# Every load waits until the load 1.75 MB ahead of it has landed

## The chip, the cores and the metric

The kernel runs on one core of a Trainium2 chip. Its five instruction queues are PE (TensorE), DVE (VectorE), ACT (ScalarE), POOL (GpSimd) and SP (SyncE); SP only issues DMAs here, and 16 DMA engines move the bytes. The metric is the device time of one execution in microseconds, as the median of several runs. Before the change it is 363.97 us (three runs, 363.48 to 364.42).

## What is computed

Three layers in a row, all in fp32, on 2304 tokens: attention with a window of 64 keys (4 sequences of 576, 8 heads of 64), a soft mixture of experts (8 experts, 4 slots each), and a feed-forward layer of width 2048. The weights of the last layer arrive as 64-bit floats.

```python
def _attn_ref(q, k, v):
    scores = scale * np.matmul(q, k.transpose(0, 1, 3, 2))
    mask = (rel >= 0) & (rel < window)
    scores = np.where(mask, scores, -1000000000.0)
    attn = np.exp(scores - np.max(scores, axis=-1, keepdims=True))
    attn = attn / (np.sum(attn, axis=-1, keepdims=True) + 1e-09)
    return np.matmul(attn, v)
...
def _moe_ref(x, phi, w1, w2):
    logits = x @ phi
    ...
    slot_input = d.T @ x          # d: softmax of the logits over the tokens
    ...
        h = np.maximum(slot_input[e] @ w1[e], 0.0)
        slot_out[e] = h @ w2[e]
    ...
    return c @ slot_out           # c: softmax of the logits over the slots
...
def _moe2_ref(x, w_in, w_out):
    h = x @ w_in
    return (h * (1.0 / (1.0 + np.exp(-1.702 * h)))) @ w_out
```

## The kernel before

The order of the work is written out by hand; a scheduler only adds the semaphore waits. There are three stages.

*Attention, up to about 90 us.* The loop `for i in range(ns)` runs over 18 pieces of work, 16 units of two heads each and two for the last chunk of every sequence. Each turn emits the scores of piece i (`emit_s`, L312 and L327), the turns of the piece before (`emit_t`, L347 and L348), its product with v (`emit_pv`, L362) and its normalization, and spread over the turns the logits and the routing sums. POOL scales q (L235) and shifts v (L243 to L250) once a load has landed. In each turn SP gets a load of q and k (`load_qk`, 512 KB, for three turns later), one of v (`load_v`, 258.5 KB) and usually one or two weight tiles (`load_w`, 1 MB). Three buffers of q/k and three of v go round, so a load of these waits until PE and POOL are done with the buffer.

*Experts, up to about 131 us.* `load_w` walks through a list, 16 tiles of w1 and then 16 of w2, 1 MB each. The w1 tiles and w2 tiles 7 to 15 go to 16 slots (`w`), the first seven w2 tiles into the memory that attention leaves (`arena`). The last w2 tile comes in three loads (`PIECES`, 512, 256 and 256 KB). PE multiplies with w1 (`emit_w1`, L786) and w2 (`emit_w2`, L824); the last two tiles are taken piece by piece (`next_w2`, L883; `last_w2`, L891), and each piece of the sum is then added (L894) and turned (`so_turn`, L899).

*Feed-forward, up to the end.* 48 steps of 36 products each (`emit_o`, L1036) on PE, with the activations on ACT and DVE. w_in and w_out come in loads of 512 KB through `raw_load` (L150), at most a few at a time.

All loads are issued by SP in program order. Every DMA uses one of eight semaphores in turn (`DMAHW0` to `DMAHW7`), and a DMA that uses a semaphore again waits until the DMA before it on that semaphore, eight places earlier, has landed. Apart from this and the buffers nothing holds a load back, so several megabytes can be issued and not landed at the same time.

Of the kernel before, what the change touches and what calls it, by code (L numbers as in the profile page):

```python
# [13 lines left out]
I32 = mybir.dt.int32  # L14
# [10 lines left out]
NU = B * NHP  # L25
# [12 lines left out]

CONV_AT = {i: n for n, i in enumerate((3, 5, 7, 9, 11))}
W = (2, 1)  # L40
N_G = 5

N_WO = 1
# [25 lines left out]
def attention_softmoe_ffn(  # L69
# [12 lines left out]
    nc = tc.nc  # L82
# [15 lines left out]
    def mem(off, n):  # L98
        return arena[:, off:off + n]
# [24 lines left out]
    def wslot(dtype=F32):  # L124
        return wp.tile([128, 4, 512], dtype, tag="w", name="w")

    def dslot(i):
        return mem(2048 * i, 2048).rearrange("p (a f) -> p a f", a=4)

    w1t, w2t = [], []  # L130
    plan = [(w1t, w1, i, None if i < N_E else i - N_E) for i in range(16)]
    plan += [(w2t, w2, i, i if i < 7 else None) for i in range(16)]
# [2 lines left out]
    def load_w(n=1):  # L135
        for _ in range(n):
            if plan:
                lst, src, i, d = plan.pop()
                t = wslot() if d is None else dslot(d)
                v = src[i].rearrange("p (a f) -> p a f", a=4)  # L140
                if not plan:
                    t, v = [x.rearrange("p a f -> p (a f)").rearrange(
                        "p (c a f) -> p c a f", c=4, a=4) for x in (t, v)]
                for c in PIECES if not plan else (slice(0, 4),):
                    nc.sync.dma_start(out=t[:, c], in_=v[:, c])
                lst.append(t)


    def raw_load(raw, src):
        nc.sync.dma_start(out=raw.bitcast(I32), in_=src.bitcast(I32))  # L150

    def widths(raw):
        r = raw.bitcast(I32).rearrange("p (n two) -> p n two", two=2)
# [35 lines left out]
    def early_load(n):  # L189
        src = w_in[n] if n < FP else w_out[n - FP]  # L190
        if wide:
            raw_load(early_raw(n), src)
        else:
            nc.sync.dma_start(out=early_dst(n), in_=src)
# [8 lines left out]
    def qbuf(n):  # L203
        return ql if n == NU else qkb[(n - (n > NU)) % 3]

    def vbuf(n):
        return vl if n == NU else vb[(n - (n > NU)) % 3]
# [14 lines left out]

    def load_qk(n):
        if n < NU:
            nc.sync.dma_start(out=qbuf(n), in_=qk[n])
        else:
            nc.sync.dma_start(out=qbuf(n)[:, 0:768], in_=sq[n - NU])

    def scale_q(n, eng):
        q = qbuf(n)  # L230
# [5 lines left out]
            out=q, in0=q, scalar1=1.0 / 8.0, scalar2=1.0, op0=ALU.mult, op1=ALU.mult)  # L236

    def load_v(n):
        nc.sync.dma_start(out=vbuf(n)[:, 0:517], in_=vt[n])

    def set_ones(n):
        v = vbuf(n)
# [2 lines left out]
    def shift_v(u):  # L245
# [6 lines left out]
            scalar1=1.0, scalar2=1.0, op0=ALU.mult, op1=ALU.mult)  # L252

    load_qk(0)
    load_qk(1)
    load_v(0)
    load_qk(2)
    load_v(1)
    nc.vector.memset(mask, 0.0)
    nc.vector.memset(pa[:, 0:128], 0.0)  # L260
# [308 lines left out]
    for b in range(B):  # L569
        g = routing(b)  # L570
        logits, lmax, dexp, turn, total, slots, gather, norm, side = g
        n = NHP * b
# [39 lines left out]
    for i in range(ns):  # L612
# [44 lines left out]
        if i == L_AT:  # L657
            load_qk(NU)
            load_v(NU)
        if i < NU:  # L660
            load_qk(i + 3 + (i + 3 >= NU))
        if i in AHEAD:
            load_w(W_AT.get(i, 0))
# [6 lines left out]
        if i not in AHEAD:  # L670
            load_w(W_AT.get(i, 0))
# [10 lines left out]
        out=ml[:, 128:160], in_=pm[0:1, 0:128].rearrange("p (t s) -> p s t", t=TM), axis=AX.X,  # L682
# [5 lines left out]
    emit_pv(ns - 1)  # L688
    emit_norm(ns - 1)
    load_w(1)  # L690

    lpt = bank("s")[:, 0:256]
    mm = sp.tile([128, 3], F32, tag="mm", name="mm")

    def tail_logits(t):
# [11 lines left out]
        out=mm[:, 2:3], in0=pm[:, 0:1], scalar1=-1.0, scalar2=None, op0=ALU.mult)  # L707
# [15 lines left out]
        out=ltt, in_=lpt, func=ACTF.Exp, bias=m, scale=1.0, accum_out=ss)  # L723
# [14 lines left out]
    for c in range(2):  # L738
        for t in range(2):
# [3 lines left out]
                start=True, stop=True, tile_position=(0, 32 * g))  # L743
# [4 lines left out]
        out=rsl, in0=pm[:, 0:1], scalar1=ss, scalar2=1e-9, op0=ALU.add, op1=ALU.add)  # L748
# [3 lines left out]
        out=i4s, in0=i4m[:, 0:NS], scalar1=rsl, scalar2=None, op0=ALU.mult)  # L752
    nc.vector.scalar_tensor_tensor(
        out=acc, in0=psl, scalar=al, in1=acc, op0=ALU.mult, op1=ALU.add)
# [85 lines left out]
    def wout_load():  # L840
        f = len(wraw)
        if f == NF:
            return
        parts_for(f)
        r = ring[f // 2 % 2][:, 1024 * (f % 2):1024 * (f % 2) + 1024]
        if wide:
            raw_load(r, w_out[f])
        else:
            nc.sync.dma_start(out=r[:, 0:512], in_=w_out[f])
        wraw.append(r)  # L850
# [10 lines left out]
    def win_more():  # L861
        n = FP + len(iraw)
        if n == NF:
            return
        if n % FP == 0:
            winf.append(gp.tile([128, 4, 512], F32, tag="wi", name="wi", bufs=2))
        iraw[n] = gp.tile([128, 1024], F32, tag="iraw", name="iraw", bufs=2)
        if wide:
            raw_load(iraw[n], w_in[n])
        else:  # L870
            nc.sync.dma_start(out=win_dst(n), in_=w_in[n])
# [99 lines left out]
    def out_w(f):  # L971
        nc.scalar.copy(whi(f), wfs[f])  # L972

    def out_c(f):
        nc.vector.tensor_tensor(  # L975
            out=wlo(f), in0=wfs[f], in1=whi(f).bitcast(F32), op=ALU.subtract)
# [18 lines left out]
    def emit_h(n, act=True):  # L995
# [4 lines left out]
        for k, a in enumerate(range(ROUND * r, ROUND * r + ROUND, PIECE)):  # L1000
            ph = bank("m")
            c = sorted({a + x for x in cuts(n, k)} | ({2048} & set(range(a, a + PIECE))))
            for c, e in zip(c, c[1:]):
                nc.tensor.matmul(  # L1004
                    ph[:, c - a:e - a], mst[:, f * 128:f * 128 + 128], cT(c, e - c),
                    start=True, stop=True)
            g = gp.tile([128, PIECE], F32, tag="g", name="g", bufs=N_G)
            gh, gl = [gp.tile([128, PIECE], F32R, tag="r", name="r", bufs=N_R) for _ in range(2)]
# [61 lines left out]
    ahead = {10: [lambda: out_w(0)], 11: [lambda: out_c(0)]}  # L1070
# [155 lines left out]
```

## Time and profile before

| | us |
|---|---|
| median of three runs | 363.97 |
| the profiled execution | 363.21 |
| its span, first to last instruction | 361.30 |
| PE busy | 351.8 (97%) |
| PE weight loads busy (beside the matmuls) | 269.7 (75%) |
| DVE / ACT / POOL busy | 240.3 / 195.5 / 45.2 |

The page counts 18,180 DMA packets and 70.87 MB. Of the DMA queues, q1 carries the loads and stores (70.38 MB), q8 ("instruction", 24 packets, 0.39 MB) and q14 ("instruction", 12 packets, 0.10 MB) the instructions of the engines. TensorE's granted clock is at its full level all through.

How to read it: busy shares are means over the span. A matmul's end is modelled, so a PE that is busy 97% need not be at its peak. A wait is shown with what ended it; "issue" means that nothing the profile shows was missing. For loads the profile gives the time from issue to landing.

### The profile page before, as it was taken

How to read it: one execution, taken by the hardware profiler on the slowest of the kernel's cores; microseconds unless marked ns; L12 is line 12 of the kernel's file. 1: busy time of each engine (PE TensorE's matmuls, PEld its weight loads, DVE VectorE, ACT ScalarE, POOL GpSimd, SP SyncE). 2: the span in 40 equal slices, each digit the busy share in tenths (PEclk: the TensorE clock that was granted, in tenths of full speed). 3: DMA queues.
4: the chain of work that ended last, by engine and by line, in shares of the span. 5: the costliest groups of instructions: out<-in, count | busy, mean ns of one | idle time of the engine just before them, and what ended most of it. 6: DMA issues, size and time to landing. Idle time of an engine off the chain costs nothing.

```text
span 361.3 us, 7742 instructions
## 1 busy us (share of the span) xinstructions
PE 351.8 (97%) x3021; PEld 269.7 (75%) x3021; DVE 240.3 (67%) x527; ACT 195.5 (54%) x499; POOL 45.2 (13%) x90
## 2 busy tenths in 40 slices
PE   8999999998999999999999999999999999999995
PEld 6787787776633357888778887788886888888884
DVE  4667797975664128885767696998787886262624
ACT  2898899877314026764757454554445553333330
POOL 4366764620100000000000000000000000000000
PEclk9999999999999999999999999999999999999999
DMA  8999999999999993333130413040300000040404
GB/s 281 407 410 406 410 411 410 402 408 406 407 417 420 415 404 130 114 117 116 58 118 32 144 47 128 11 139 27 116 2 0 0 2 1 0 175 1 174 3 174
DMA packets 18180, 70.87 MB, mean 196 GB/s; under 512 B 2016, under 2 KB 2400, under 8 KB 14176
## 3 DMA queue, kind: packets, MB, share of 16 engines
q1 hardware_dynamic: 18144, 70.38, 50.6%
q8 instruction: 24, 0.39, 0.4%
q14 instruction: 12, 0.10, 0.1%
HBM read 65.65 MB, written 4.72 MB: 195 GB/s over the span
## 4 chain that ended last, share of the span: by engine, by line
PE 92%; ACT 2%; DVE 2%; issue 1%; DMA 1%; DVEq 0%; ACTq 0%
PE s L1036 18%; PE t L1036 18%; PE v L1036 18%; PE v L362 5%; PE m L1004 5%; PE m L347 5%; PE s L327 4%; PE s L786 4%; PE v L824 3%; PE s L312 2%; PE m L400 2%; ACT pa L339 1%; PE m L441 1%; PE m L491 1%; DMA rawt<-in_qk_dram 1%
## 5 line engine op out<-in xcount | busy, mean ns | idle before, releaser
L992 ACT ACTIVATE r<-m 128x384 fp32r<-128x384 f32 (+1 forms) x97 | 47.4, 492 | 80.6 <-PE m L1004 80.4
L1017 DVE TENSOR_TENSOR r<-g,r 128x384 fp32r<-128x384 f32 x96 | 51.4, 554 | 48.4 <-ACT g L992 40.0
L1036 PE MATMUL t<-w,r 128*128 128x512 f32 x288 | 75.8, 395 | 0.0
L1036 PE MATMUL s<-w,r 128*128 128x512 f32 x288 | 74.3, 393 | 0.0
L1036 PE MATMUL v<-w,r 128*128 128x512 f32 (+1 forms) x291 | 73.3, 387 | 0.0
L1036 PEld LDWEIGHTS t<-w,r 128*128 128x128 f32 x288 | 53.8, 188 | 14.8 <-issue 4.0
L1036 PEld LDWEIGHTS v<-w,r 128*128 128x128 f32 x291 | 54.4, 188 | 11.3
L1036 PEld LDWEIGHTS s<-w,r 128*128 128x128 f32 x288 | 52.6, 188 | 8.5
L992 ACT ACTIVATE g<-m 128x384 f32<-128x384 f32 x96 | 47.9, 500 | 0.0
L339 ACT ACTIVATE pa<-s,nm 128x128 f32<-128x128 f32 x140 | 40.9, 404 | 5.6 <-DVE nm L332 5.6
L332 DVE TENSOR_REDUCE nm<-s 128x4 f32<-128x512 f32 x35 | 22.5, 684 | 5.6 <-PE s L327 4.9
L1004 PE MATMUL m<-cT,w 128*128 128x384 f32 (+2 forms) x113 | 25.9, 320 | 0.0
L1004 PEld LDWEIGHTS m<-cT,w 128*128 128x128 f32 x113 | 20.8, 188 | 4.9 <-ACT g L992 0.7
L347 PE MATMUL m<-ident,pa 128*128 128x128 f32 x144 | 20.9, 283 | 0.8 <-ACT pa L339 0.4
L347 PEld LDWEIGHTS m<-ident,pa 128*128 128x128 f32 x144 | 15.6, 141 | 5.1 <-issue 1.8
L348 ACT COPY pa<-m 128x512 f32<-128x512 f32 x18 | 10.7, 596 | 10.4 <-PE m L347 10.4
L786 PE MATMUL s<-w,phis 128*32 128x512 f32 x128 | 14.6, 595 | 0.0
L972 ACT CAST w<-wf 128x512 fp32r<-128x512 f32 x15 | 9.3, 623 | 9.3 <-DVE wf L175 9.3
L381 DVE TENSOR_TENSOR arena<-v,rs 128x256 f32<-128x256 f32 x36 | 13.6, 419 | 0.6
L327 PE MATMUL s<-arena 64*64 64x128 f32 x352 | 13.8, 271 | 0.1
L975 DVE TENSOR_TENSOR w<-wf,w 128x512 fp32r<-128x512 f32 x15 | 10.3, 689 | 5.2 <-ACT w L972 5.1
L1056 DVE TENSOR_TENSOR w<-s,w 128x512 f32<-128x512 f32 x18 | 11.6, 684 | 2.8 <-PE s L1036 2.8
(218 smaller groups left out, 453.0 us busy)
## 6 DMA issues: line engine op xcount, KB each, us to landing
w<-in_w_dram SPq DMA_DIRECT2D x24, 1024.0 KB, 9.6
w<-in_w_out_dram SPq DMA_DIRECT2D x16, 512.0 KB, 3.4
arena<-in_w_dram SPq DMA_DIRECT2D x7, 1024.0 KB, 10.8
iraw<-in_w_in_dram SPq DMA_DIRECT2D x12, 512.0 KB, 3.3
arena<-in_qk_dram SPq DMA_DIRECT2D x10, 512.0 KB, 8.8
out_dram<-w SPq DMA_DIRECT2D x16, 256.0 KB, 2.1
arena<-in_vt_dram SPq DMA_DIRECT2D x13, 258.5 KB, 7.3
rawt<-in_qk_dram SPq DMA_DIRECT2D x6, 512.0 KB, 8.8
```

The lines of the kernel that those rows point to most:

```text
L327: nc.tensor.matmul(st[h][rows[j], c, :], q, k, start=False, stop=(c == 3), tile_position=(64 * h, 64 * j))
L332: nc.vector.tensor_reduce(out=nm[:, h], in_=st[h], axis=AX.X, op=ALU.max, negate=True)
L339: nc.scalar.activation(out=pb[h][:, c, :], in_=st[h][:, c, :], func=ACTF.Exp, bias=nm[:, h, c:c + 1], scale=1.0)
L347: nc.tensor.transpose(tt[:, c, :], pb[h][:, c, :], ident)
L362: nc.tensor.matmul(pvt[i][h][64 * j:64 * j + 64, c, :], ab[h][:, c, 64 * j:64 * j + 64], v, start=True, stop=True, tile_position=(0, 64 * j))
L381: nc.vector.tensor_tensor(out=o, in0=pv[h][:, :, 1 - h:65 - h], in1=rs[:, h].unsqueeze(2).to_broadcast([128, 4, 64]), op=ALU.mult)
L786: nc.tensor.matmul(ph[32 * j:32 * j + 32, :], siT[:, kk, :], w1t[4 * r + j][:, kk, :], start=(kk == 0), stop=(kk == KD - 1), tile_position ...
L992: nc.scalar.activation(out=(gh, g)[part][:, a:e], in_=ph[:, a:e], func=ACTF.Gelu_apprx_sigmoid)
L1004: nc.tensor.matmul(ph[:, c - a:e - a], mst[:, f * 128:f * 128 + 128], cT(c, e - c), start=True, stop=True)
L1017: nc.vector.tensor_tensor(out=gl, in0=g, in1=gh.bitcast(F32), op=ALU.subtract)
L1036: nc.tensor.matmul(accs[t][:, h], a[:, c], b[:, h], start=(first and k == 0), stop=(last and k == 2 and h.stop == 512))
L1056: nc.vector.tensor_tensor(out=o[:, h], in0=accs[t][:, h], in1=o[:, h], op=ALU.add)
```

## The change

A helper `start` now issues the loads of q/k, v and weights. It keeps a list of the loads issued so far with their bytes. For a new load it goes back through the list from the newest, adding up bytes; the first load that has at least `AHEAD_OF` = 1,750,000 bytes of listed loads between itself and the new one becomes a dependency: the new load's issue waits until that one has landed. `raw_load` goes through `start` as long as the list has fewer than `LAST` = 79 entries. `FREE` is 0, so the rule holds from the first load that has so much ahead of it. The load of phi is not on the list, nor are the loads after the last piece of w2 or the stores.

```diff
+AHEAD_OF = 1750000
+FREE = 0
+LAST = 79
...
+    queue = []
+
+    def start(out, in_):
+        x = nc.sync.dma_start(out=out, in_=in_)
+        ahead = 0
+        for y, n in reversed(queue):
+            if ahead >= AHEAD_OF and len(queue) >= FREE:
+                tc.add_manual_dep(x.ins, y.ins.name, mybir.DependencyInfo(
+                    mybir.DependencyClass.Sync, mybir.DependencyReason.DATA), reason="depth")
+                break
+            ahead += n
+        queue.append((x, int(np.prod([k for _, k in out.ap])) * 4))
+
...
-                    nc.sync.dma_start(out=t[:, c], in_=v[:, c])
+                    start(t[:, c], v[:, c])
...
-        nc.sync.dma_start(out=raw.bitcast(I32), in_=src.bitcast(I32))
+        (start if len(queue) < LAST else nc.sync.dma_start)(out=raw.bitcast(I32), in_=src.bitcast(I32))
...
-            nc.sync.dma_start(out=qbuf(n), in_=qk[n])
+            start(qbuf(n), qk[n])
...
-            nc.sync.dma_start(out=qbuf(n)[:, 0:768], in_=sq[n - NU])
+            start(qbuf(n)[:, 0:768], sq[n - NU])
...
-        nc.sync.dma_start(out=vbuf(n)[:, 0:517], in_=vt[n])
+        start(vbuf(n)[:, 0:517], vt[n])
```

The instructions of all five queues stay in their order; only waits on SP differ. At the end of the attention SP issues the last w1 tiles (`w` from `in_w1`), the last two v loads and the first w2 tiles (into `arena`). Before, in SP's queue:

```order
L145 DMA w_1589<-in_w1_dram 128x2048 [waits DMAHW1_49,DVE_49,Activation_49]
L239 DMA arena_78<-in_vt_dram 128x517 [waits DMAHW2_49,PE_49,Pool_49]
L239 DMA rawt_91<-in_vt_dram 128x517 [waits DMAHW3_49,PE_49,Pool_49]
L145 DMA w_1675<-in_w1_dram 128x2048 [waits DMAHW4_49,DVE_49,Activation_49]
L145 DMA w_1677<-in_w1_dram 128x2048 [waits DMAHW5_49,DVE_49,Activation_49]
L145 DMA arena_78<-in_w2_dram 128x2048 [waits DMAHW6_49]
```

and after:

```order
L136 DMA w_1589<-in_w1_dram 128x2048 [waits DMAHW4_49,DVE_49,Activation_49]
L136 DMA arena_78<-in_vt_dram 128x517 [waits DMAHW7_49,PE_49,Pool_49]
L136 DMA rawt_91<-in_vt_dram 128x517 [waits PE_49,Pool_49]
L136 DMA w_1675<-in_w1_dram 128x2048 [waits DVE_49,Activation_49]
L136 DMA w_1677<-in_w1_dram 128x2048 [waits DMAHW0_49,DMAHW5_49,DVE_49,Activation_49]
L136 DMA arena_78<-in_w2_dram 128x2048 [waits DMAHW6_49,DMAHW3_49]
```

No row moves. Where a row had the semaphore of the load eight places earlier, it now has that of a nearer load, or none where an earlier row waits for the same one. By the byte counts, `w_1677` waits for the w1 tile five loads before it (`w_1587`), and the first `arena` tile for the v load into `rawt_91`, two loads before `w_1677`.

The second place is the last w2 tile and the first w_out load behind it. SP's queue before:

```order
L145 DMA w_2004<-in_w2_dram 128x2048 [waits DMAHW4_49,PE_49]
L145 DMA w_2031<-in_w2_dram 128x1024 [waits DMAHW5_49,PE_49]
L145 DMA w_2031<-in_w2_dram 128x512 [waits DMAHW6_49]
L145 DMA w_2031<-in_w2_dram 128x512 [waits DMAHW7_49]
L150 DMA w_2091<-in_w_out_dram 128x1024 [waits DMAHW0_49,PE_49]
```

and after:

```order
L136 DMA w_2004<-in_w2_dram 128x2048 [waits DMAHW1_49,PE_49]
L136 DMA w_2031<-in_w2_dram 128x1024 [waits DMAHW2_49,PE_49]
L136 DMA w_2031<-in_w2_dram 128x512
L136 DMA w_2031<-in_w2_dram 128x512 [waits DMAHW3_49]
L166 DMA w_2091<-in_w_out_dram 128x1024 [waits PE_49]
```

Again nothing moves: the last piece of w2 now waits for the w2 tile four loads before it, and the w_out load has no wait on a DMA of its own any more.

## Rows read from the trace of the kernel before

**Rows 1.** Stretches: us, busy (x count) of PE, PEld, DVE, ACT, POOL; PEclk, DMA, GB/s.
```profile
2.00:90.00 88.00, 85.32 (x1593) 67.90 (x1593) 64.60 (x187) 70.64 (x221) 42.24 (x81) 1.00 1.02 404
...
100.00:126.00 26.00, 26.00 (x231) 8.85 (x234) 10.99 (x24) 5.60 (x10) 0.19 (x1) 1.00 1.01 418
...
150.00:200.00 50.00, 50.00 (x231) 40.66 (x230) 37.04 (x69) 33.74 (x73) 0.00 (x0) 1.00 0.27 90
```
**Rows 2.** Waits of PE: line waited for, us in total, times, longest.
```profile
PE v L362 <- issue: 1.7, 1, 1.7
```
**Rows 3.** Timeline of PE: start, us, what, [idle before, what ended it].
```profile
90.41 0.22 PE L362 MATMUL v<-arena,pl 128*64 128x65 f32 x1 [1.70 <-issue]
```
**Rows 4.** Timeline of ACT just before that stall.
```profile
87.59 0.59 ACT L348 COPY pl<-m 128x512 f32<-128x512 f32 x1
```
**Rows 5.** Two stretches from one instruction block's arrival to the next, columns as rows 1.
```profile
48.70:55.10 6.40, 6.40 (x127) 5.39 (x129) 6.16 (x19) 5.56 (x17) 5.41 (x9) 1.00 1.04 417
...
81.90:90.40 8.50, 6.81 (x123) 5.63 (x124) 4.91 (x18) 6.30 (x21) 0.21 (x2) 1.00 1.01 410
```
**Rows 6.** DMA queues (packets, MB, share): q8 79.3:79.5; q1, q14 79.5:87.7; q8 87.7:87.9.
```profile
q8 instruction: 1, 0.02, 33.8%
...
q1 hardware_dynamic: 666, 3.29, 100.3%
q14 instruction: 1, 0.01, 0.2%
...
q8 instruction: 1, 0.02, 33.7%
```
**Rows 7.** Timeline of SP's DMA issues: start, us, destination and source, count.
```profile
73.35 1.62 SPq L145 DMA_DIRECT2D w<-in_w_dram  x2
...
80.52 0.33 SPq L239 DMA_DIRECT2D rawt<-in_vt_dram  x1
80.95 0.85 SPq L145 DMA_DIRECT2D w<-in_w_dram  x2
81.85 1.08 SPq L145 DMA_DIRECT2D arena<-in_w_dram  x2
...
95.55 2.14 SPq L145 DMA_DIRECT2D arena<-in_w_dram  x3
...
103.74 0.33 SPq L145 DMA_DIRECT2D w<-in_w_dram  x1
...
115.69 0.33 SPq L145 DMA_DIRECT2D w<-in_w_dram  x1
```
**Rows 8.** Issue to landing (last number, us), issues at 73.4, 80.5, 81.0, 81.4, 81.9, 95.6, 103.7, 115.7.
```profile
w<-in_w_dram SPq DMA_DIRECT2D x1, 1024.0 KB, 8.6
...
rawt<-in_vt_dram SPq DMA_DIRECT2D x1, 258.5 KB, 5.2
...
w<-in_w_dram SPq DMA_DIRECT2D x1, 1024.0 KB, 7.3
...
w<-in_w_dram SPq DMA_DIRECT2D x1, 1024.0 KB, 9.3
...
arena<-in_w_dram SPq DMA_DIRECT2D x1, 1024.0 KB, 11.4
...
arena<-in_w_dram SPq DMA_DIRECT2D x1, 1024.0 KB, 7.7
...
w<-in_w_dram SPq DMA_DIRECT2D x1, 1024.0 KB, 6.9
...
w<-in_w_dram SPq DMA_DIRECT2D x1, 256.0 KB, 15.1
```
**Rows 9.** Timeline of PE's weight loads (PEld) at the last piece of w2.
```profile
131.46 0.24 PEld L891 LDWEIGHTS v<-w,rawt 128*32 128x32 f32 x8
132.14 0.63 PEld L899 LDWEIGHTS t<-i,acc 128*128 128x128 f32 x5 [0.45 <-DVE acc L894]
```
**Rows 10.** Timeline of POOL: first use of the last v load.
```profile
85.87 0.11 POOL L243 MEMSET rawt<- 128x5 f32 x1 [0.57 <-DMA rawt<-in_vt_dram]
```
**Rows 11.** Part 6 of the page: loads issued one by one in the feed-forward part.
```profile
iraw<-in_w_in_dram SPq DMA_DIRECT2D x12, 512.0 KB, 3.3
```

## What I predict, and why

> **What bounds the kernel now.** I read the table of stretches first. The 16 DMA engines are full while the attention runs (2 to 90 us) and in the stretch of 1 MB weight loads, at 404 and 418 GB/s [rows 1]. PE computes there almost without a break. So up to 131 us there are two bounds side by side, PE and the stream of loads. Later, as in 150 to 200 us, the DMA engines are busy for a quarter of the time and PE for all of it [rows 1]; this change adds no wait there.
>
> Next the list of PE's waits. It has one stall of a size that matters: 1.7 us, and what ended it is "issue" [rows 2], so nothing that the profile shows was missing. The timeline puts it before 90.41 us, between the two halves of the last P·V of the attention (L362) [rows 3]. The data were there: ScalarE copied the operand `pl` at 87.59 for 0.59 us, so from 88.2 us on it could be read [rows 4]. What PE lacked is best seen in the DMA queues. The queue q8, "instruction", moved one block of 16 KB at 79.3 to 79.5 us, none from 79.5 to 87.7, and one at 87.7 to 87.9 [rows 6]. Its share there, 33.7% of 16 engines over 0.2 us, is 1.1 us on one engine, so that block ended at about 88.9 us, and 1.5 us later PE went on. Between such blocks PE starts about 256 instructions: 127 + 129 in 48.7 to 55.1 us, 123 + 124 in 81.9 to 90.4 us (matmuls and weight loads together) [rows 5]. My reading: PE's instructions come through the DMA engines that carry the loads, and at 88.7 us PE had run out of them because a block came late.
>
> **What the change adds.** 79 loads are put on a list, all but phi up to the last piece of w2. 73 of them get a wait on the newest load that has at least 1.75 MB of listed loads between itself and them. With the sizes of this kernel that leaves 1.84 to 2.76 MB in between: 1.84 MB where a q/k load (0.52), a v load (0.26) and a weight load (1.05) alternate, 2.10 MB among 1 MB weights. No work is added or moved on PE, DVE, ACT or POOL, and SP's DMAs keep their order. Behind a waiting load on SP stand all later loads, the ones that attention needs too.
>
> *The loads themselves: 0 us.* A load in a full stream lands when the bytes ahead of it have landed, however early it was issued. The condition is that the stream never runs dry. 1.84 MB at 404 GB/s are 4.5 us of work. Against that stands the time from a landing to new data. Issued into an idle stream, 512 KB land after 3.3 us [rows 11], of which 0.524 MB at 410 GB/s are 1.3 us, so 2.0 us go by before data flow, and an issue of 0.33 to 0.42 us comes on top: 2.4 us. In the full stream there is a case close to the limit: of the three loads issued one after the other from 95.55 us on, the first had landed (7.7 us later, at 103.25) when SP issued the next load, at 103.74 [rows 7, 8]. So two loads, 2.1 MB, were ahead of it. It lands after 6.9 us, at 110.6: 3.15 MB in the 7.4 us from 103.25 on are 426 GB/s, and nothing ran dry. Bounds of this term: 0 us, and the third rival if the cover of 2.1 us (4.5 - 2.4) does not hold. I take 0, as the row with 2.1 MB ahead is nearest.
>
> *The queue in front of the instruction block: up to 1.70 us.* At about 81.9 us (79.4 + 1.1 + 1.5, the previous block's arrival by the same reckoning) PE can ask for the next one. Before, SP had by then issued weight loads at 80.95 and directly after, and another at 81.85 [rows 7]; they land 7.3, 9.3 and 11.4 us after issue, at 88.2, 90.7 and 93.2 us [rows 8]. The block began at 87.8 us, between the landings of the first two. In the changed kernel the second (issued about 81.4) waits for the landing of the weight load issued at 73.35, 8.6 us later, at 81.9 to 82.0 [rows 7, 8], and the third waits for the v load issued at 80.52, which lands 5.2 us later, at 85.7. So at 81.9 us up to two loads fewer, 1.0 to 2.1 MB, stand in front of the block: 2.5 to 5 us of stream. PE needs 1.7 us of that for the stall to vanish. Bounds: 0 us, if the block does not queue behind loads or asks after 82.0, and 1.70 us, the whole stall. I take the upper end, since the block's wait of 5.9 us (81.9 to 87.8) is about two such loads at 2.5 us each, and those are what moves. The wait before the other blocks shortens likewise, but what follows caps the gain.
>
> *What is late next: the load stream, which gives back 0.7 us.* The last piece of w2 is issued at 115.69 and lands 15.1 us later, at 130.8 [rows 7, 8]. Its landing does not move (the first term). From a landing to the first use 0.1 to 0.2 us pass, and I take 0.1: the v load of 80.52 + 5.2 = 85.7 us, used by POOL at 85.87 [rows 7, 8, 10]. Now the weight loads of that piece (L891 into `v`) start at 131.46 and take 0.24 us, and the next step on PE, the turn of the result (L899), starts at 132.14 [rows 9]. PE takes its work in order, so L899 cannot start before 130.8 + 0.1 + 0.24 = 131.14: at most 1.00 us earlier. Of 1.70 us, 1.00 reach the end, 0.70 turn into a wait of PE for the last pieces of w2. Beyond L899 all is work of PE that shifts as a whole.
>
> **Sum.** The profiled execution took 363.21 us (span 361.30 and 1.91 around it): 363.21 - 1.70 + 0.70 = 362.21. It lies 0.76 us below the median of the three timed runs, so I set the gain against the median: 363.97 - 1.00 = **363.0 us**.
>
> On one rule. The rows say only that the block of 87.8 us began 8.4 us after the one before it. The Trainium skill, "DMA: Bandwidth & Descriptors", section "Queues, rings and completion order", says that each DMA engine goes round its queue rows packet by packet. By that rule a block of instructions would wait for a packet or two of loads, however many are queued; a shorter load queue would change nothing, and the sum would be 0, not -1.00. This result is the first rival, worked out below from rows.
>
> **Rivals.** (1) *No effect.* The block is asked for late or takes turns with the loads, so the 5.9 us do not depend on the queue; or it asks after 82.0 us, when the second load is again in front. The stall stays, and the load stream stays: 363.97 - 0 = 364.0 us. For it: no row shows when the block was asked for. Against it: the wait is as long as two weight loads. The Trainium skill, "Runtime: NRT & Kernel Launch", section "Instruction fetch mechanics", calls the cost of crossing a block mostly hidden; the stall of 1.70 us is a place in this trace where it is not.
> (2) *The stream gets faster too.* With fewer loads open at once, the attention part could run nearer the 418 GB/s of the weight stretch. 88 us at 404 instead of 418 GB/s are 88 x 14/418 = 2.9 us; a quarter of it, 0.7 us, lifts the cap, and the whole stall comes back: 363.97 - 1.70 = 362.3 us. For it: the difference in rate is there. Against it: those 88 us also hold the smaller rows of q, k and v, which would explain the rate as well.
> (3) *The stream runs dry (slower).* The place is SP's wait in front of each load. It decides once the time from a landing to new data exceeds the 4.5 us that lie queued. Up to 131 us the stream moves about 53 MB (404 GB/s for 88 us and about 418 for 41). One dry spell per 1.84 MB is 29 spells; with 0.1 us each, 2.9 us. The cover is the 131.46 - 130.9 = 0.6 us by which the last piece is early now: 363.97 + 2.9 - 0.6 = 366.3 us, and worse with every further tenth. For it: 73 waits, each on a whole load. Against it: 2.4 us are needed where 4.5 are there.
> That the waits do nothing since others come first is part of (1): among SP's waits before the change are those on the DMA eight places earlier.
>
> **How the numbers follow.** Forecast 0.60: 363.0, by the bounds of its terms 362.6 to 363.5. Rival (1) 0.16: 364.0. Rival (2) 0.12: 362.3. Rival (3) 0.12: 366.3. A measurement of this kernel can tell about 0.3% from no change, 1.1 us, so the border of faster is 362.9, close to the forecast. I count 0.24 of its 0.60 as beyond it and 0.36 as within. Faster: 0.24 + 0.12 = 0.36. Same: 0.36 + 0.16 = 0.52. Slower: 0.12. The range leaves out rival (3) and the far end of (2), and takes in (1) with the spread of the runs shown (about 0.5 us to either side): 362.1 to 364.6.
>
> **What would show it.** Right: the stall before the second half of L362 is gone or under 0.3 us; q8's block lies well before 87.7 us; SP's weight loads that were issued at 81.85 us and later come 4 to 10 us later, while the last piece of w2 still lands at 130.8 within 0.5 us; a new wait of PE's weight loads for a DMA of w at L883 or L891, about 0.7 us together; DMA share still full to 136 us. Wrong: the stall stays though the queue is shorter (rival 1); the last w2 piece lands before 130.1 (rival 2) or after 131.5 us (rival 3); waits of POOL or PE on q, k or v that grow in the attention part; a second stall on "issue" at another place.

## The result, and the profile after

The changed kernel is slower by half a percent: 365.73 us (median of 20 runs) against 363.44 us of the kernel before in the same series (20 runs), a ratio of 1.0052 with an interval of 1.003 to 1.0075. All ratios here are taken over the fast executions alone (two of these 20 ran in a slower state of the chip), so they are not quite the ratios of the medians. The profiled execution took 364.88 us with a span of 363.0 us, 1.7 us more than before. The line numbers used here are 16 higher than before, so L362 is now L378, L891 is L907 and L899 is L915; every load of the list is issued at L136.

The waits of PE in the changed kernel (line waited for, us in total, times, longest), to be set beside [rows 2]:

```profile
PE v L378 <- issue: 1.7, 1, 1.7
...
PE s L343 <- POOL arena L259: 0.8, 1, 0.8
PE m L899 <- DMA w<-in_w_dram: 0.5, 1, 0.5
```

The stall that was to vanish is there with its old size. Two other waits of 0.5 us or more are new: one for POOL, which scales q once its load has landed, and one for a load of w. The two stretches up to 126 us, columns as in [rows 1]:

```profile
2.00:90.00 88.00, 84.42 (x1593) 67.27 (x1593) 64.17 (x187) 70.77 (x221) 42.57 (x81) 1.00 1.01 394
100.00:126.00 26.00, 26.00 (x229) 8.97 (x232) 11.00 (x24) 5.81 (x11) 0.44 (x1) 1.00 1.01 407
```

In the attention the stream moves 394 GB/s instead of 404. Over 88 us that is 88 x 10/404 = 2.2 us of stream. The DMA share is still 1.01, so the share does not show the loss; the rate does. The last piece of w2 (a load of 256 KB, issued at 128.35 us) shows where it ends:

```profile
w<-in_w_dram SPq DMA_DIRECT2D x1, 256.0 KB, 5.1
```

It lands at 133.5 us, 2.7 us later than before (115.69 + 15.1 = 130.8 [rows 7, 8]), though the time from issue to landing fell from 15.1 to 5.1 us. PE's weight loads at that place, to be set beside [rows 9]:

```profile
133.52 0.16 PEld L907 LDWEIGHTS v<-w,rawt 128*32 128x32 f32 x8 [0.51 <-DMA w<-in_w_dram]
133.88 0.74 PEld L915 LDWEIGHTS t<-i,acc 128*128 128x128 f32 x6 [0.20 <-DVE acc L910]
```

L915 starts at 133.88 us where L899 started at 132.14: 1.74 us, the whole difference of the spans. From 82 us on, the chain that ended last is the new one, a load, SP's issue, the next load (start, us, what):

```profile
82.22 7.84 DMA w<-in_w_dram
...
90.14 7.41 DMA arena<-in_w_dram
...
97.62 8.22 DMA arena<-in_w_dram
...
105.91 7.47 DMA w<-in_w_dram
...
113.44 7.41 DMA w<-in_w_dram
...
120.92 7.42 DMA w<-in_w_dram
...
128.35 5.13 DMA w<-in_w_dram
133.48 0.04 issue
133.53 0.42 PE v L907 x8
133.95 0.66 PE t L915 x4
```

Note the 8.22 among values of 7.41 to 7.47 (the first load of the chain has more bytes ahead of it): one step of 0.8 us, and nothing lost behind it. A block of q8 came at 97.3 us, just before that load was issued. The experiments below say what such a step is. Last, the queues at the place of the stall: q8 at 78.6 to 78.8 us, all queues at 78.9 to 88.1, q8 at 88.1 to 88.3, to be set beside [rows 6]:

```profile
q8 instruction: 1, 0.02, 34.3%
...
q1 hardware_dynamic: 748, 3.71, 100.0%
q14 instruction: 1, 0.01, 0.2%
...
q8 instruction: 1, 0.02, 34.4%
```

PE's block of instructions comes at 88.2 us, no earlier than before (87.8).

### The profile page after: what moved, and what is told of

Read it like the earlier page. It is cut to its first block, busy times and chain, and to the rows that moved or that the text cites. A ratio compares the mean times of both kernels' runs of the same rounds, so it can differ in the third digit from the quotient of the medians.

```text
span 363.0 us, 7748 instructions
## 1 busy us (share of the span) xinstructions
PE 351.6 (97%) x3021; PEld 268.8 (74%) x3021; DVE 240.0 (66%) x527; ACT 195.7 (54%) x499; POOL 45.6 (13%) x90
## 4 chain that ended last, share of the span: by engine, by line
PE 78%; DMA 15%; ACT 2%; DVE 1%; issue 1%; POOL 1%; DVEq 0%; SPq 0%; ACTq 0%; POOLq 0%
PE s L1052 18%; PE t L1052 18%; PE v L1052 18%; DMA w<-in_w_dram 10%; PE m L1020 5%; DMA arena<-in_w_dram 4%; PE v L378 4%; PE m L363 4%; PE s L343 4%; PE s L328 2%; ACT pa L355 2%; PE m L416 2%; DMA rawt<-in_qk_dram 1%; PE m L934 1%; PE m L507 1%
```

## Experiments: where the stream loses its time

The first theory (A) was that the short queue ties the 16 DMA engines together. A wait ends when the slowest engine has delivered its part, and by then the others have little or nothing left to do; so what holds up one engine, such as a block of instructions, holds up the whole stream. The rivals were that every wait of SP costs something by itself (B; the prediction's third rival has this form), and later that single loads of the attention simply run dry (D). After the run with one wait (e7), A was put in numbers and is called S in the expectations. Loads are numbered in the order of SP's queue from 0 on; phi, number 5, is not on the list, so a number in the code is one lower than the load's.

**Distance and place.** Four kernels change the distance or the range of the waits.

```
-AHEAD_OF = 1750000
+AHEAD_OF = 3000000      (e1_3mb)
+AHEAD_OF = 1250000      (e2_125mb)
...
-            if ahead >= AHEAD_OF and len(queue) >= FREE:
+            if ahead >= AHEAD_OF and FREE <= len(queue) < 50:   (e3_first50)
...
-FREE = 0
+FREE = 55               (e4_from55)
```

> AHEAD_OF is 3,000,000 instead of 1,750,000 bytes, nothing else. Theory A (the 16 DMA engines are coupled: with a short queue, an engine that makes a detour to fetch an instruction block holds up the whole stream, as the other engines run out of loads; a longer queue lets them run ahead): the last piece of w2 lands at 130.5 to 131.7 us instead of 133.5, and the time is within 0.3% of the kernel before. Theory B (the waits themselves cost time on SP, some hundredths of a microsecond for each of 73 loads): the last piece still lands at 133 to 134 us and the time stays about 0.5% above before.

> AHEAD_OF is 1,250,000 bytes. Theory A: the attention part, where 1.31 to 1.84 MB are then ahead, is coupled more tightly; its loads come 2 to 4 us later than with 1.75 MB, the last piece of w2 lands at 135 us or later and the time is 1 to 1.5% above before. Theory B: as with 1.75 MB, 133 to 134 us and about 0.5%.

> AHEAD_OF 1.75 MB, but only the first 50 loads of the list wait (to the middle of the last third of the attention). Theory A: the stream keeps the 1.2 us that it had lost by then (the weight load issued at 67.5 us landed at 74.6 instead of 73.4), and loses little after: the last piece of w2 lands at 131.4 to 132.6 us; time 0.1 to 0.4% above before. If the loss belonged to the weight stretch alone, the last piece would land at 130.8.

> AHEAD_OF 1.75 MB, but only from the 56th load of the list on (the last weight tiles of w1, the last two v loads and all of w2). Theory A: only the instruction blocks after about 80 us are passed on to the stream; with 1.75 MB from the start these cost about 0.8 us, so the last piece of w2 lands at 131.2 to 132.0 us; time 0 to 0.3% above before. The stall of PE before the second half of the last P.V stays at 1.5 to 2 us if the instruction block's wait does not depend on what is queued beyond two loads; it falls below 0.5 us if it does.

| kernel | ratio to before, interval | GB/s, 2 to 90 us | last piece of w2 lands |
|---|---|---|---|
| before | 1 | 404 | 130.8 |
| 3 MB (e1) | 0.9992 [0.9959, 1.0024] | 402 | 131.5 |
| 2.25 MB (e9, below) | 0.9978 [0.9946, 1.0009] | 401 | 131.4 |
| 1.75 MB (the change) | 1.0052 [1.003, 1.0075] | 394 | 133.5 |
| 1.25 MB (e2) | 1.0393 [1.0344, 1.0442] | 338 | 148.5 |
| 1.75 MB, first 50 listed loads (e3) | 1.0043 [1.0011, 1.0075] | 390 | 133.8 |
| 1.75 MB, from the 56th listed load on (e4) | 0.9998 [0.9972, 1.0025] | 400 | 131.1 |

The rates and landings are those of one profiled execution each. Up to load 63 the kernel before, e10, e12 and e13 have the same loads and waits, and that load lands at 95.7, 96.6, 96.0 and 97.0 us. So a difference of about 1 us in one landing says nothing by itself, and the verdicts rest on the ratios.

At 3 MB the waits are still there (SP issues the last piece of w2 at 122.3 us instead of 115.7) and cost nothing that can be measured, so B falls. The waits of the attention alone bring the whole loss (e3, more than expected), those of the 1 MB weights none (e4; 2.1 MB or more lie ahead of all but the last piece there, not 1.84). In e4 PE's stall at the last P·V stays too, at 1.4 us, as it should if the block's wait does not depend on loads queued further back. At 1.25 MB the loss is three times what was expected, and PE's wait for POOL, which scales q, is now the largest:

```profile
PE s L343 <- POOL arena L251: 3.2, 3, 1.2
```

**Detours, a test that failed.** Eight small extra loads on POOL's queue were meant as models of instruction blocks, in the kernel before (e5) and in the changed one (e6).

```
     nc.gpsimd.memset(ht[:, 0:LS0], 0.0)
+    for n in range(8):
+        nc.gpsimd.dma_start(out=scratch, in_=w1[n][0:17, 0:256])
```

> The kernel before, with eight small extra loads on GpSimd's queue, one after the other from about 100 us on, in the stretch of 1 MB weight loads: each brings 17 rows of 1 KB into a tile that nobody reads, as a model of the blocks of instructions that pass through the DMA engines beside the loads. Theory A (in the short queue of the changed kernel every hold-up of one DMA engine holds up all of them, since the wait is for the slowest of 16 engines and the others have little left to do; in the deep queue of the kernel before the others run on): the last piece of w2 lands at 130.8 to 131.6 us, little moved. Theory D (the attention part of the changed kernel loses time because single loads of 0.26 and 0.5 MB run dry, whatever else passes through the engines): the same. This run is the measure for the next one.

> The changed kernel (1.75 MB) with the same eight small extra loads. In its stretch from 106 to 128 us no time was lost against the kernel before. Theory A: the last piece of w2 moves by 1 to 4 us against 133.5 us in the changed kernel, and by more than it moves in the kernel before. Theory D: it moves by no more than in the kernel before, under 0.8 us.

The last piece of w2 landed at 131.7 us (0.9 later than before, just outside what was expected) and at 133.5 us (not moved), ratios 1.0001 [0.996, 1.0042] and 1.0067 [1.0026, 1.0108]. By the letter that speaks against A. But the extra load is no model of a block: the queue of e5 at 104.0 to 104.45 us shows one of them.

```profile
q0 software_dynamic: 15, 0.02, 9.8%
```

9.8% of 16 engines over 0.45 us are 0.71 us of work, more than one engine can do in 0.45 us; so several engines shared it, where a block of 16 KB is one packet that keeps one engine busy for 1.1 us. The pair says nothing on A.

**One wait by itself (e7).** The kernel before, in which only the load that was issued at 80.95 us waits, for the v load directly ahead of it.

```
-            if ahead >= AHEAD_OF and len(queue) >= FREE:
+            if len(queue) == 59:
```

> The kernel before with a single wait: the weight load that is issued at 80.95 us waits for the v load directly ahead of it (landing 85.76), so that nothing new comes into the DMA queue while PE's block of instructions is due. It measures two steps of the prediction by themselves. The time from a landing to new data, put at 2.4 us: the stream is dry for 2.3 to 2.6 us, and the last piece of w2 lands at 133.0 to 133.5 instead of 130.8 us. The wait of the instruction block: if it stands behind the loads that are queued when PE asks for it (step of the prediction), q8's block starts by 86.5 us and the stall of 1.7 us on L362's counterpart is under 0.5; if its wait does not depend on that queue, or if it is asked for later than reckoned (82 us), it starts at 87.3 to 88.3 us and the stall is 1.3 to 1.8 us. The time is about 365.0 us (+1.0 to +2.0) by both, since the last piece of w2 sets the end.

The timeline of SP has the held load at 86.16 us; the table of stretches (columns as in [rows 1]) shows the stream thin behind that:

```profile
86.16 0.80 SPq L136 DMA_DIRECT2D w<-in_w_dram  x2
```
```profile
86.10:87.90 1.80, 1.80 (x36) 1.41 (x27) 1.10 (x4) 1.80 (x7) 0.11 (x1) 1.00 0.43 73
```

The DMA queues show its time from issue to landing, and q8's block at 85.4 to 85.7 us; the waits of PE show the stall nearly gone:

```profile
w<-in_w_dram SPq DMA_DIRECT2D x1, 1024.0 KB, 4.8
...
q8 instruction: 1, 0.02, 21.8%
```
```profile
PE v L378 <- issue: 0.3, 1, 0.3
```

So the time from a landing to new data was right: of the 4.8 us, 2.5 are the load's own bytes (1.05 MB at 418 GB/s), which leaves 2.3, and with 0.15 us of waking and issuing 2.4. But the last piece of w2 landed at 135.0 us, 4.2 us later and not 2.4, and the time rose by 1.03% [0.7, 1.36]. The trace's landing events (each load ends in 16 parts) show the rest. Before the wait, the first and the last part of a load lay 2.5 us apart: some engines ran ahead of the slowest. When the slowest had delivered the v load, the leading engines had been idle for up to 2.5 us already; between the first parts of the two landings 4.5 us are missing, between the last parts 2.4. The held load then landed with 0.4 us between its parts: the lead was gone. The next block of instructions (93.2 us) found all engines level, and the load landing then (the one issued at 87.02) was 1.3 us late. These two losses, 2.4 and 1.3 us, make up most of the 4.2; 0.3 were there before the wait.

**One load ahead (e8, e10).** Nine, then thirteen waits on 1 MB weights in the kernel before.

```
-            if ahead >= AHEAD_OF and len(queue) >= FREE:
+            if 59 <= len(queue) < 68 and ahead >= 1000000:   (e8)
+            if 63 <= len(queue) < 76 and ahead >= 1000000:   (e10)
```

> The kernel before with nine waits: the loads numbered 60 to 68 in the order of the queue (1 MB weights, first use from 104 us on) wait until only one load of 1.05 MB, 2.5 us of work, is left between them and the load they wait for. By the prediction's reckoning (2.4 us from a landing to new data) nothing runs dry: load 68 lands at 108.2 to 108.8 us as before. If the lag between the fastest and the slowest of the 16 DMA engines (2.3 to 3.1 us by the landings' first and last parts) comes on top, since the wait is for the slowest: 1.5 to 2.5 us are lost at each of the first waits, less once the engines run level, 5 to 15 us by load 68. The last piece of w2 moves by the same amount.

> The kernel before with thirteen waits, the loads numbered 64 to 76 (1 MB weights): each waits until one load of 1.05 MB, 2.6 us of work, is left between it and the load it waits for. By the prediction's reckoning (2.4 us from a landing to new data) nothing runs dry, and the last piece of w2 lands at 130.8 to 131.3 us. By theory S the lag of the engines is used up at the first waits, and from then on each of the three blocks of PE's instructions that pass in that stretch (about 96, 106 and 121 us) holds up the whole stream by its 1.1 us or a little more: the last piece lands at 133.0 to 135.0, and the loss stands in two or three steps at these blocks, not evenly at thirteen loads. If it stands evenly, single loads take longer than reckoned to bring data.

e8 took 369.59 us (ratio 1.0133 [1.0049, 1.0218]), but in its profiled execution PE stood still for 2.9 us in the attention, before any of the nine waits, and the stream ran dry there:

```profile
PE s L343 <- issue: 3.6, 2, 2.9
```

Its landings cannot be set against those of the kernel before, so it decides nothing; e10 repeats it further on. There the time rose by 0.94% [0.54, 1.33] and the last piece of w2 landed at 135.7 us, later than any theory had it. The issue-to-landing times have two levels (loads issued at 102.15, 110.77 and 118.25 us):

```profile
arena<-in_w_dram SPq DMA_DIRECT2D x1, 1024.0 KB, 6.1
...
w<-in_w_dram SPq DMA_DIRECT2D x1, 1024.0 KB, 4.9
...
w<-in_w_dram SPq DMA_DIRECT2D x1, 1024.0 KB, 6.5
```

The blocks of q8 came at 103.9 and 120.4 us, within the two slow loads. Between them the loads from 108.2 to 118.2 us land 2.5 us apart, as in the kernel before, though only one lies ahead. So the loss is not spread over the waits. Steps of 1.0 and 1.4 us stand at the two blocks, one of 0.4 at the block before them (94.0 us), which still found a lead of 2.5 us, and one of 0.7 behind the last wait, with no block near it. Of the 4.9 us by which the last piece is late, 0.9 were there before the first wait, and 0.5 are spread over steps of 0.2 us or less.

**More blocks (e12, e13).** Whether the blocks are the cause was tested by doubling them: the matmuls of the two expert products are cut into halves, in the kernel before (e12) and in e10 (e13).

```
+    CUT = (slice(0, 256), slice(256, 512))
...
+                for c in CUT:
+                    nc.tensor.matmul(
+                        ph[32 * j:32 * j + 32, c], siT[:, kk, :], w1t[4 * r + j][:, kk, c],
...
+            for c in CUT:
+                nc.tensor.matmul(
+                    po[32 * j:32 * j + 32, c], ht_of(i, j), w2t[i][:, j, c],
...
```

> The kernel before with the 240 matmuls of the two expert products (L786, L824) cut into halves of 256 columns: the same sums, some 480 PE instructions more between 97 and 131 us, so about two blocks of instructions more pass through the DMA engines there. With the queue as deep as before, theory S lets the other engines run on while one brings a block: the last piece of w2 lands at 130.6 to 131.8 us. If a block holds up the stream whatever is queued, it moves by 1.1 us for each, to 132.5 or later.

> The same halves, with the thirteen waits of the run with one load ahead (its last piece of w2 landed at 135.71 us). By theory S each further block of instructions costs its 1.0 to 1.4 us: two more put the last piece at 137.3 to 138.8 us, and the steps between landings of 1 MB that exceed 2.5 us stand at the blocks, as many as there are blocks. If the steps of that run had another cause (a place in the program, a certain load), their number does not grow and the last piece stays within 0.7 us of 135.7.

Both have four blocks of q8 between 97 and 131 us instead of two. In e13 they lie in the stretches of 1.1 us from 105.7, 112.4, 121.0 and 130.0 us on, one in each:

```profile
q8 instruction: 1, 0.02, 5.4%
...
q8 instruction: 1, 0.02, 5.4%
...
q8 instruction: 1, 0.02, 5.6%
...
q8 instruction: 1, 0.02, 5.5%
```

And these are its loads issued at 99.53, 102.12, 108.34, 110.84, 116.95, 119.43, 125.53 and 128.03 us, each from issue to landing (last number):

```profile
arena<-in_w_dram SPq DMA_DIRECT2D x1, 1024.0 KB, 5.0
...
arena<-in_w_dram SPq DMA_DIRECT2D x1, 1024.0 KB, 6.2
...
w<-in_w_dram SPq DMA_DIRECT2D x1, 1024.0 KB, 4.9
...
w<-in_w_dram SPq DMA_DIRECT2D x1, 1024.0 KB, 6.0
...
w<-in_w_dram SPq DMA_DIRECT2D x1, 1024.0 KB, 4.9
...
w<-in_w_dram SPq DMA_DIRECT2D x1, 1024.0 KB, 6.0
...
w<-in_w_dram SPq DMA_DIRECT2D x1, 1024.0 KB, 4.9
...
w<-in_w_dram SPq DMA_DIRECT2D x1, 1024.0 KB, 6.4
```

They take 4.9 to 5.0 us where no block passes and 6.0 to 6.4 where one does: four blocks, four steps (1.3, 1.1, 1.1 and 1.5 us by the landings), where e10 had two. (A load issued before such a step is over also takes 6.0 to 6.2 us, but lands 2.5 us after the one before it. A fifth block, at 94.9 us, came while the lead was still 2.6 us, and left no step.) The last piece of w2 landed at 137.0 us, a little under the expected 137.3. With the 1.2 us by which load 63 was late before the first wait, the four steps are the whole 6.2 us by which that piece is late. With the deep queue of e12, three of the four blocks left no step; one, at 128 us, left 1.2 us, and its last piece landed at 132.2 us, 0.4 above what was expected. One execution of each took 363.62 (e12) and 368.97 us (e13), beside one of the kernel before with 362.46. So it is shown that blocks of instructions hold up a queue with one load ahead, nearly all of them and by their own 1.1 us or a little more, and a deep one seldom.

That the lead of some engines makes the difference, and not the depth of the queue as such, shows in e7 and in e11 (below). In both the one wait is over and about 4 MB are queued again when the next block comes, at 93.2 and 88.1 us. But the lead is down to 0.5 us, and the load that is next to land comes 1.3 and 1.1 us late. The block at the same place in the kernel before (87.8 us, a lead of 2.6 us) leaves nothing, and the later blocks of e7 and e11, at leads of 1.6 us and more, leave 0.3 us at most. No run set the lead by itself.

**2.25 MB (e9).** What must lie queued is then 2.4 us plus the lead of the fastest engines, mostly 1.8 to 3.1 us by the landing parts of the kernel before and the changed one: 4.2 to 5.5 us. The change leaves 1.84 MB, 4.5 us, in the attention; 2.25 MB leave at least 2.36 MB, 5.8 us.

```
-AHEAD_OF = 1750000
+AHEAD_OF = 2250000
```

> The changed kernel with 2.25 MB instead of 1.75: between a load and the one it waits for lie at least 2.36 MB, 5.8 us of work at 410 GB/s. Theory S (a wait is released by the slowest of the 16 DMA engines; the fastest is by then out of work for the lag between them, 1.8 to 3.1 us by first and last part of a landing, on top of the 2.4 us from a landing to new data, which the run with one wait measured; so 4.2 to 5.5 us must lie queued, where the changed kernel has 4.5): the last piece of w2 lands at 130.8 to 131.8 us, and the time is within 0.25% of the kernel before. If every wait had a cost of its own, or the loss fell slowly with the distance, it would land at 132 us or later.

The last piece of w2 landed at 131.4 us, and the time is that of the kernel before (0.9978 [0.9946, 1.0009]). The loss does not fall off slowly with the distance; half a megabyte more removes it.

**Back to the changed kernel.** Its own landings can be set against the time that the bytes of each load take in a stream that does not run dry (2.5 us for 1 MB). From load 20 on it loses 4.9 us in this way and the kernel before 1.8; 0.4 us of the difference are a start that was so much earlier, the rest are the 2.7 us. Six of the 13 blocks of q8 between 26 and 122 us (33.3, 40.4, 51.9, 65.3, 78.7 and 97.3 us) are followed by a landing that is 0.5 to 0.9 us late, 4.1 us together. In the kernel before two are (65.1 and 73.1 us, 1.2 and 0.4 us). In the attention the lead is 1.5 to 2.6 us in the changed kernel and 1.9 to 3.5 us before (loads 20 to 55). Theory D accounts for little: a load that runs dry is late with its first part as with its last, and only one (load 35, 0.4 us) is. But not every step has a block beside it: in e3, where the attention has the same waits nearly to its end, one of 0.9 us at 32.6 us has none before it. So blocks are the larger part of the loss; that they are all of it is not shown.

## Experiments: what the instruction block waits for

e7 has answered half of it: with no load at hand, the block comes at 85.5 us, as the v load ends. e11 puts that one load between the two cases: it is held back until a VectorE reduction ends, so its data should come just in time. For that the load and the one behind it are written one turn later in the program (`W_AT`), after the reduction; SP's order stays the same.

```
-W_AT = {**{i: 1 for i in range(2, 17)}, 12: 0, 15: 2, 16: 2, 17: 3}
+W_AT = {**{i: 1 for i in range(2, 17)}, 12: 0, 15: 2, 16: 0, 17: 5}
...
+        if len(queue) == 59:
+            tc.add_manual_dep(x.ins, reds[-2].ins.name, mybir.DependencyInfo(
+                mybir.DependencyClass.Sync, mybir.DependencyReason.DATA), reason="place")
```

> The kernel before with the weight load that was issued at 80.95 us held back until a reduction of VectorE ends (83.25 us), the loads behind it after it. Its data should still come before the v load ahead of it has landed (85.8), so that the slowest engine does not run dry. If PE's block of instructions asked for its place before 83.3 us, it stands in front of this load: q8's block starts at 85.3 to 86.3 us instead of 87.8, the stall before the second half of the last P V is under 0.5 us instead of 1.7, and the last piece of w2, at 130.8 to 132.0, becomes the bound (PE waits 0.5 to 1.5 us for it): the time is 363.0 to 364.2, no more than 0.3% from the kernel before. If the block asks later, or its wait has nothing to do with that load, it starts at 87.5 us or later and the stall stays at 1.3 to 1.8 us.

SP issued the load at 83.94 us, a little later than reckoned (timeline of SP). q8's block came at 88.1 us (DMA queues at 88.0 to 88.3 us; none lies in 81.3 to 88.0), and the stall stayed, at 1.2 us, a little under what was expected (waits of PE; the traces of e1, e3, e4, e9, e10 and e12 have 1.2 to 1.4 there):

```profile
83.94 1.04 SPq L136 DMA_DIRECT2D w<-in_w_dram  x2
```
```profile
q8 instruction: 1, 0.02, 20.2%
```
```profile
PE v L374 <- issue: 1.4, 2, 1.2
```

| kernel | this load issued at | q8's block begins at | longest stall on issue at the last P·V |
|---|---|---|---|
| before | 80.95 | 87.8 | 1.7 |
| changed | 82.22 | 88.2 | 1.7 |
| e11 | 83.94 | 88.1 | 1.2 |
| e7 | 86.16 | 85.5 | 0.3 |

In these runs the block lets exactly this one load go first, whether it was issued at 80.95 or as late as 83.94 us. In the kernel before three more were issued by 82.6 us, and the block did not wait for those. So the block does not stand in one line behind all that SP has issued. By these four cases it waits for the load that is under way or next, and comes early only if there is a hole. What fixes its place, and when PE asks for it, stays open. That the stall follows the block, as the prediction read it, is borne out by e7: the block came 2.3 us earlier than before, and 0.3 us of the stall were left. As a version e11 gains nothing: 0.999 [0.9964, 1.0016]. Its last piece of w2 comes at 132.8 us, so the stream would take back what a shorter stall gives.

## Why the prediction was wrong, point by point

**What bounds the kernel: right.** PE and the load stream lie side by side up to 131 us. In the changed kernel the stream alone sets the end of that part.

**The loads themselves, "0 us": wrong, and this is the step that decided.** The response of 2.4 us was right (e7: 2.4). The condition "the stream never runs dry" was taken for the stream as a whole, with 4.5 us queued against 2.4. But 16 engines do not run level. The wait is for the last of them, and the first are mostly ahead by 1.8 to 3.1 us, so 4.2 to 5.5 us are needed if they are to keep that lead. Where they lose it, the next block of instructions is no longer covered (e7, e11, e13); with 5.8 us queued the loss is gone (e9). The row that the prediction leaned on, the issue at 103.74 us with two loads ahead [rows 7, 8], has 2.1 MB ahead and lies in the weights, where e4 finds no loss either; it was carried over to the attention, where mostly 1.84 MB lie ahead and a block passes every 6.4 to 8.5 us [rows 5]. The term measured +2.7 us at the last piece of w2.

**The queue in front of the instruction block, "up to 1.70 us": wrong, 0.** The rows already held the answer: the prediction put the block "between the landings of the first two" loads, but it began at 87.8 us, before even the first had landed at 88.2 [rows 6, 8]. So only that load was in front, and the gate holds back the two behind it. The lower bound ("does not queue behind" all issued loads) was the one to take; e11 and e7 show it. For this term the outcome is that of rival 1. The Trainium skill, "DMA: Bandwidth & Descriptors", section "Queues, rings and completion order", has each engine change queues only after a whole packet, typically of 9 to 17 descriptors. What the prediction drew from that rule, that a shorter load queue changes nothing for the block, came out. How long such a packet takes, no run shows. e7 against e11 (85.5 and 88.1 us) shows that the block can let a whole load of 1 MB, 2.5 us, go first. The traces list such a load as nine records on each engine; if a record is one descriptor, that can be one packet, so the load in front does not speak against the rule.

**What is late next: right as a rule, with the opposite sign in use.** L899 cannot start before the last piece of w2 + 0.1 + 0.24 us. With 133.48 that gives 133.82, and L915 started at 133.88. The rule was meant to cap a gain, and it passed on a loss: of 2.7 us in the stream 1.74 reach the end, as 2.7 less the same 1.00 us that the cap had; rival 3 had put this cover at 0.6.

**The rivals.** Rival 3 (slower, 366.3 us) came: its mark, a last piece after 131.5 us, and nearly its time, 365.73. Its place was right (SP's wait), its price was about right in sum (2.9 us against 2.7) and wrong in kind: not 29 spells of 0.1 us, but mostly six steps of 0.5 to 0.9 us behind blocks of instructions (4.1 us, where the kernel before loses 1.6 at two blocks). That its time came so near is in part luck: the 0.1 us a spell came from no row, and 1.0 us was covered, not 0.6. It had 0.12; the range ended at 364.6 us, below the result. Rival 2 (a faster stream) is refuted: 394 GB/s.

**The marks.** The loads that SP issued from 81.85 to 86.5 us before came 5.7 to 7.5 us later, as expected; those after them came 2.1 to 14.2 us later, beyond the mark on both sides. PE's wait for w at the last tiles came, with 0.5 us on PE and 1.4 us on its weight loads, where 0.7 was expected. The waits on POOL, a named mark of being wrong, came as well, but they cost only 0.25 us by the last P·V (90.66 against 90.41 [rows 3]).

## What to carry to other kernels

When a load waits for an earlier one, set what lies between them against the time from a landing to new data plus the lead of the fastest DMA engine over the slowest (here 2.4 and mostly 1.8 to 3.1 us); the time alone is not enough, and the DMA share stays full while the rate falls. Where a queue has been deep, that depth also covers whatever stops a single engine, such as instruction blocks; count those per stretch and price each at its own length before shortening the queue. And when a stall is to be cured by taking work out of a queue, check by the landing times which piece of it the stalled one really followed.

## What the runs showed of the hardware

- A block of PE instructions (16 KB, about 256 instructions) takes about 1.1 us of one DMA engine. With one 1 MB load ahead it makes the load then under way land 1.1 to 1.5 us late (4.9 against 6.0 to 6.4 us, e13); with a deep queue three of four left no mark (e12). The Trainium skill, "Runtime: NRT & Kernel Launch", section "Instruction fetch mechanics", calls the cost of crossing a block mostly hidden. It speaks of the engine that fetches; the loads beside it pay in these runs, 1.1 to 1.5 us a block with one load ahead (e13).
- A wait that empties the stream once costs more than the empty time: 2.4 us of emptiness and 1.3 us more at the next block (e7), before which the lead of the other engines had fallen from 2.5 to 0.5 us.
- Issued into an idle stream, 1 MB lands after 4.8 us, 2.3 us more than its bytes take (e7).
